# One core: logit sums on GpSimd, conversion steps gathered, a new order at batch ends and tail

## The chip, the cores and the metric

The kernel runs on one core of one Trainium2 chip. The metric is the device time of one execution in microseconds (us), and every time below is in us unless it is marked ns. The engines of a core are TensorE (PE in the profile, its weight loads PEld), VectorE (DVE), ScalarE (ACT), GpSimd (POOL) and SyncE (SP), which here issues the DMAs.

## The reference

Attention with pooled queries, then a soft mixture of experts, then a two-layer block whose activation is a smooth hinge. All tensors are float32.

```
q_pool = q.reshape(B, H, S // 2, 2, D).mean(axis=3)         # B=4, H=8, S=1152, D=64
attn   = softmax(q_pool @ k^T / sqrt(D)) @ v                # 576 rows per head
x      = attn, heads side by side                           # 2304 tokens x 512

logits = x @ phi                                            # 32 slots: 8 experts x 4
d      = softmax(logits, over tokens);   c = softmax(logits, over slots)
slot   = d^T @ x                                            # 32 x 512
so[e]  = relu(slot[e] @ w1[e]) @ w2[e]                      # w1 512 x 1024, w2 1024 x 512
y      = c @ so                                             # 2304 x 512

h = y @ w_in                                                # 512 x 2048
g = 0 below -1, h above 1, (h + 1)^2 / 4 between
out = g @ w_out                                             # 2048 x 512
```

## The kernel before

**Attention.** The 32 heads (4 batches of 8) are worked off in 16 pairs, P = 0 to 15, the two heads of a pair in the two halves of the PE array. The 1152 keys are 9 blocks of 128, so step g = 9 P + c is block c of pair P, and each step has two half-slots (one for each head). In a half-slot TensorE makes the scores in fp16 for the maximum (tile `mx`, L311, four products), the exact scores (`st`, L377) and, for an earlier block, exp times values (`acc`, L409). VectorE takes the row maximum of `mx` (`mp`, L323), ScalarE the exponential (`e`, L382). VectorE also adds the exponentials of several blocks (`es_add`, L390; which ones, in which half-slot and how wide is the table ADD), so that one set of products (`es_sum`, L402) makes the sums of a pair at its end; `es_sum` is the first thing in the trace that belongs to the start of the next pair.

In the same half-slots stand the preparation of later pairs (table PREP): loads of k and q, splits into two fp16 parts (L266, L279, L289 on VectorE), transposes by DMA (L272, L294, L360), a copy of the transposed q to the other 64 partitions (`dup_q1`, L297, a DMA), and, between them, the conversion of the last block's weights (`cv_step`: L207, L209, L212, L215, four steps on VectorE for each piece of 512 columns; table CVS says in which half-slots of a pair they go). After a pair its outputs are transposed and multiplied by phi (`t_x`, L449), scaled (`t_raw`, `t_ev`, `t_mul` on ScalarE) and left in `XL`: for each head and each of five token blocks 64 values and 32 logits.

**Batch end.** A batch is four pairs. In the third pair after its last one, the logits of its eight heads are added (`lg_red`, L489, three reductions on VectorE), then their maximum over tokens is found (`lg_mx`, `lg_tr`, `lg_max`), spread over the partitions (`lg_rep`), exponentiated (`lg_exp`) and multiplied with the tokens (`p_mm`), and the running sums are updated (`p_add`). The last batch does the same behind the last pair, with no attention left beside it.

**Order.** Nothing is reordered behind the code: `plan()` puts each step into a half-slot with `at(g, slot, f, ...)`, the half-slots are emitted in turn, and each engine and each DMA queue works its instructions in the order in which they were emitted. All loads go through SP's queue.

**Tail.** Behind the last batch's chain come the slot inputs (`sT`), the first layer of the experts (`h1`, L741; its 16 weight tiles of 1 MB are w1[e, x]; w1[1, 0] is loaded last, as `w_last`, into memory that the batch chain has to free), the softmax over slots on VectorE (`c_soft`, L763 to L774), the second layer (`s2o`, L798, weights w2), and the product of its result with `w_in` (`M`, L905, then `Mr`, `Mst`).

**Output stage.** For groups of tokens k: `c_xpose(k)` (tile `ct`, L786) makes the transposed coefficients, `h_unit` multiplies them with M (`h`, L927), ScalarE and VectorE form the hinge (`g_unit`, L935 to L948; the first ones in `first_unit`, L973 to L980, where GpSimd subtracts in L980), and `o_part` multiplies with w_out (`po`, L991). The tiles `h` and `ct` share four PSUM buffers.

Of the kernel before, what the change touches and what calls it, by code (L numbers as in the profile page):

```python
# [19 lines left out]
WARM = 2, 2, 3, 2, 6, 3  # L20
# [5 lines left out]
CVS = ((0, 0), (0, 0), (0, 1), (1, 1)), ((0, 0), (0, 0), (0, 1)), ()  # L26
# [7 lines left out]
ADD = (((5, 1, 0, 0, 2), (6, 1, 1, 0, 2), (7, 2, 1, 0, 1), (8, 2, 0, 0, 1), (8, 2, 1, 1, 2), (9, 2, 0, 1, 2),  # L34
        (10, 3, 1, 0, 2), (11, 3, 0, 0, 2), (12, 4, 0, 0, 1), (13, 4, 0, 1, 2), (13, 4, 1, 0, 1), (14, 4, 1, 1, 2), (15, 5, 0, 0, 2),
# [3 lines left out]
PREP = (-20, -18, (-34, -33), -36, -16, -30), (-24, -22, (-37, -36), -37, -17, -32)  # L39
# [3 lines left out]
def fused_kernel(ctx: ExitStack, tc: tile.TileContext, q, k, v, phi, w1, w2, w_in, w_out, out):  # L43
# [420 lines left out]
    def t_last(P, part):  # L464
        def px(h, t):
            i, k = place(t, h)
            return tx[P][:, i, BW * k:BW * k + BW]

        for h in range(2):
            for t in range(NTT):  # L470
                sc = ss[P][:, h, t:t + 1]
                if part == 0:
                    x = LG[:, NTT * (P // HPB) + t, :]
                    nc.vector.scalar_tensor_tensor(out=x, in0=px(h, t)[:, D:BW], scalar=sc, in1=x, op0=ALU.mult, op1=ALU.add)
                elif part == 1 and 2 <= t:
                    nc.scalar.activation(out=xl_of(P, h, t)[:, 0:D], in_=px(h, t)[:, 0:D], func=AF.Copy, scale=sc)
                elif part == 2 and t < 2:
                    nc.vector.tensor_scalar(out=xl_of(P, h, t)[:, 0:D], in0=px(h, t)[:, 0:D], scalar1=sc, scalar2=None, op0=ALU.mult)
# [130 lines left out]
    with tc.manual_schedule():  # L609
# [117 lines left out]
        def over_slots(ps, src):  # L727
            for dc in range(4):
# [32 lines left out]
        def c_soft(i):  # L761
# [55 lines left out]
        c_soft(0)
        for i in range(3):
            if i:
                h1(4 + i, 0)  # L820
            c_soft(1 + i)
        nc.gpsimd.memset(hz1, 0.0)
        h1(7, 0)
        nc.scalar.activation(out=h1s[0], in_=h1p[0][:, 0], func=AF.Copy)
        h1(0, 1)
        h1(1, 1)
        h1(2, 1)
# [53 lines left out]
        nc.vector.tensor_copy(S2sb, s2)  # L881
# [162 lines left out]
        m_rep(0)  # L1044
        w_hi(0, 0)
# [11 lines left out]
        for k in range(len(SEQ)):  # L1057
            if k:
                pos = o_tiles(k)
            if k == 0:  # L1060
# [12 lines left out]
                c_xpose(3)  # L1073
# [79 lines left out]
```

## Time and profile before

| | |
|---|---|
| median of 3 runs | 768.32 us (764.88 to 768.39) |
| profiled execution | 767.93 us, of which its span 766.2 us |
| granted TensorE clock, mean | 0.982 |
| busy: PE, DVE, ACT, POOL | 731.4 (95%), 595.4 (78%), 460.9 (60%), 108.0 (14%) |
| chain of work that ended last | PE 58%, DVE 30%, issue 5%, DMA 4%, ACT 2% |

The span is the time from the first instruction to the last in the trace; the time of the execution is 1.7 us longer. An engine's share of busy time is a mean over stages with different limits, and TensorE's busy time counts a product as longer when its input or its turn comes late. The chain is followed back from the last instruction, at each step to what released it.

### The profile page before, as it was taken

Reading aid. Unit: us, or ns where it says so; the run is one execution under the profiler, and the core shown is the slowest. Engines: PE = TensorE matmul, PEld = TensorE weight load, DVE = VectorE, ACT = ScalarE, POOL = GpSimd, SP = SyncE. Lnnn points to the kernel's source line nnn. Section 1 sums busy time; section 2 is a strip of 40 time slices with the busy share of each in tenths; the row PEclk is TensorE's granted clock in tenths of the full one; section 3 lists DMA queues with packets and bytes.
Section 4 is the critical chain, followed back from the end, with each engine's and each line's share of the span. In section 5 each row is a group of like instructions: output and inputs, shape, how many; then the busy total and the mean of one; then the engine's idle time right before and its main releaser. Section 6 shows DMA issues by size and latency. Waiting matters only on the chain.

```text
span 766.2 us, 19663 instructions
## 1 busy us (share of the span) xinstructions
PE 731.4 (95%) x8138; PEld 569.4 (74%) x8138; DVE 595.4 (78%) x1104; ACT 460.9 (60%) x880; POOL 108.0 (14%) x78
## 2 busy tenths in 40 slices
PE   7789999999999998999999999799899999999998
PEld 6567788786787786788866786524788888888887
DVE  6889898889899889889879778432666798887542
ACT  4245667656667756657755568112878678667650
POOL 7100000000000000000000000001434434335350
PEclk9899999999999999999999999799999999999999
DMA  9698499766598876559775567997101220210122
GB/s 217 124 229 191 111 224 225 155 184 173 133 205 222 159 173 181 132 149 246 151 165 121 160 212 241 345 385 293 55 1 53 86 79 32 83 56 1 58 94 97
DMA packets 135258, 118.75 MB, mean 155 GB/s; under 512 B 81153, under 2 KB 99841, under 8 KB 134657
## 3 DMA queue, kind: packets, MB, share of 16 engines
q1 hardware_dynamic: 135168, 117.50, 58.3%
q8 instruction: 64, 1.05, 0.6%
q14 instruction: 26, 0.20, 0.1%
HBM read 82.90 MB, written 8.91 MB: 120 GB/s over the span
## 4 chain that ended last, share of the span: by engine, by line
PE 58%; DVE 30%; issue 5%; DMA 4%; ACT 2%; SPq 1%; DVEq 0%; ACTq 0%
PE po L991 25%; DVE mp L323 12%; DVE es L390 10%; PE st L377 7%; PE acc L409 6%; PE acc L402 5%; PE tx L449 4%; PE mx L311 3%; PE h L927 2%; PE s2o L798 2%; PE h L741 1%; DMA q<-q 1%; DMA w_last<-in_moe_w_dram 1%; DVE qn L289 1%; DVE xT L489 1%
## 5 line engine op out<-in xcount | busy, mean ns | idle before, releaser
L382 ACT ACTIVATE e<-st 128x576 f32<-128x576 f32 x288 | 187.2, 651 | 118.6 <-PE st L377 104.2
L323 DVE TENSOR_REDUCE mp<-mx 128x1 f32<-128x576 f32 x282 | 210.7, 749 | 43.2 <-PE mx L311 42.4
L409 PE MATMUL acc<-e,vf 128*64 128x288 f32 x1152 | 201.4, 408 | 1.6 <-ACT e L382 1.6
L311 PE MATMUL mx<-K,q 128*64 128x288 f16 x1152 | 125.6, 291 | 11.2 <-DVE mp L323 4.3
L377 PE MATMUL st<-q,K 128*64 128x288 f16 x1152 | 129.3, 288 | 7.4 <-DVE mp L323 5.5
L377 PE MATMUL st<-q,S 128*64 128x288 f16 x1152 | 129.4, 286 | 0.1
L311 PEld LDWEIGHTS <-q 128*64 128x64 f16 x1152 | 76.4, 111 | 64.4 <-issue 8.3
L991 PE MATMUL po<-whi,ghi 128*128 128x512 f32 x280 | 110.2, 394 | 0.0
L991 PE MATMUL po<-wlo,ghi 128*128 128x512 f32 x280 | 110.2, 394 | 0.0
L991 PE MATMUL po<-whi,glo 128*128 128x512 f32 x280 | 110.0, 393 | 0.0
L390 DVE TENSOR_TENSOR es<-es,e 128x288 f32<-128x288 f32 (+1 forms) x190 | 103.9, 560 | 0.0
L960 POOL TENSOR_TENSOR glo<-r,ghi 128x1024 fp32r<-128x1024 f32 x34 | 81.8, 2406 | 118.8 <-DVE r L948 76.6
L377 PEld LDWEIGHTS <-K 128*64 128x64 f16 x1152 | 74.4, 109 | 26.5 <-issue 16.1
L409 PEld LDWEIGHTS acc<-e,vf 128*64 128x64 f32 x1152 | 82.9, 137 | 9.3 <-ACT e L382 4.4
L377 PEld LDWEIGHTS <-S 128*64 128x64 f16 x1152 | 75.9, 110 | 1.3 <-issue 0.4
L1003 DVE TENSOR_TENSOR pa<-po,pa 128x512 f32<-128x512 f32 (+1 forms) x54 | 36.9, 682 | 39.7 <-PE po L991 39.5
L720 POOL MEMSET xT<- 128x1024 f32 x1 | 1.0, 957 | 461.5 <-PE tx L449 461.5
L991 PEld LDWEIGHTS po<-whi,glo 128*128 128x128 f32 x280 | 52.9, 189 | 11.8
L991 PEld LDWEIGHTS po<-whi,ghi 128*128 128x128 f32 x280 | 52.9, 189 | 11.1 <-ACT cl L945 0.2
L991 PEld LDWEIGHTS po<-wlo,ghi 128*128 128x128 f32 x280 | 52.9, 189 | 10.2
L948 DVE SCALAR_TENSOR_TENSOR r<-h,cl 128x512 f32<-128x512 f32 x68 | 43.6, 682 | 8.5 <-ACT cl L944 6.9
L462 ACT ACTIVATE xl<-xl,ss 128x96 f32<-128x96 f32 x150 | 47.1, 366 | 0.0
(185 smaller groups left out, 860.1 us busy)
## 6 DMA issues: line engine op xcount, KB each, us to landing
w<-in_moe_w_dram SPq DMA_DIRECT2D x76, 256.0 KB, 4.5
w<-in_moe_w_dram SPq DMA_DIRECT2D x12, 1024.0 KB, 11.5
vf<-in_v_dram SPq DMA_DIRECT2D x16, 576.0 KB, 4.3
kf<-in_k_dram SPq DMA_DIRECT2D x30, 288.0 KB, 4.0
f<-in_moe_w_in_dram SPq DMA_DIRECT2D x16, 512.0 KB, 4.9
f<-in_moe_w_out_dram SPq DMA_DIRECT2D x16, 512.0 KB, 3.7
qf<-in_q_dram SPq DMA_DIRECT2D x30, 256.0 KB, 5.0
S<-K SPq DMA_DIRECT2D x16, 288.0 KB, 4.7
```

The costliest lines, as they stand in the source:

```text
L311: nc.tensor.matmul(ps[p0:p1, i, 0:HQ], lhsT=q1[P][:, t, p0:p1], rhs=kk[:, j * HQ:(j + 1) * HQ], start=True, stop=True)
L323: nc.vector.tensor_reduce(out=mp[P][:, t, a:a + 1], in_=ps[:, :, 0:HQ], op=ALU.max, axis=AX.XY)
L377: nc.tensor.matmul(ps[c0:c0 + 64, i, 0:HQ], lhsT=kk[:, ci, c0:c0 + 64], rhs=f[:, sl[i]], start=first, stop=not first)
L382: nc.scalar.activation(out=e, in_=ps[:, :, 0:HQ], func=AF.Exp, scale=ESC)
L390: nc.vector.tensor_tensor(out=Es[P, n, h][:, i0:i1], in0=a[:, i0:i1], in1=b[:, i0:i1], op=ALU.add)
L402: nc.tensor.matmul(acc[P, h][32 * r:32 * r + 32, HQ:HQ + SW], lhsT=ones.to_broadcast([128, 32]), rhs=a, start=False, stop=False, skip_grou ...
L409: nc.tensor.matmul(acc[P, i][h * 64:(h + 1) * 64, 0:HQ], lhsT=vt[P][:, h, c, :], rhs=E[P, c, h][:, i, :], start=(c == 0), stop=(c == NK - ...
L462: nc.scalar.activation(out=x, in_=x, func=AF.Copy, scale=ss[P][:, h, t:t + 1])
L948: nc.vector.scalar_tensor_tensor(out=r[:, a:a + 2], in0=ps[a // 2], scalar=-1.0, in1=cl[:, a:a + 2], op0=ALU.max, op1=ALU.add)
L960: nc.gpsimd.tensor_tensor(out=glo[k], in0=r, in1=ghi[k].bitcast(F32), op=ALU.subtract)
L991: nc.tensor.matmul(ps, lhsT=a, rhs=b, start=st_, stop=sp)
L1003: nc.vector.tensor_tensor(out=t, in0=po, in1=t, op=ALU.add)
```

## The change

- The sum of the logits over a batch's heads (`lg_red`, three VectorE reductions per batch) is gone. In its place `lg_add` runs on GpSimd once for each pair but the last: three instructions for a batch's first pair, four for the others. The mask `dupm` is added there too, so `lg_exp` has one VectorE instruction instead of two. `lg_mx` to `lg_exp` stand one half-slot later.
- CVS: the four conversion steps of a pair stand in its first half-slot; before they were spread over three. Pairs from 9 on had three steps, now four.
- ADD: 12 instead of 14 additions for the same blocks, the first one half-slot earlier.
- PREP and `plan`: the loads of q are emitted one half-slot later, the low part of q one later.
- Behind the last pair, `t_last` makes head 0's logits on VectorE, head 1's outputs and head 0's values on ScalarE, and adds with two VectorE instructions; filling products (`warm`) are more or in other places.
- At the start, the memory fills of `S2b` and `qn2b` are divided otherwise between VectorE and GpSimd.
- In the tail `h1` uses `w_last` behind twelve other tiles instead of four, and `c_soft`'s last two steps run on ScalarE and GpSimd.
- `c_xpose(3)` moves from behind group 0's products to right behind `m_rep(0)`; the copy of `S2sb` is shared by VectorE and ScalarE.

```diff
-WARM = 2, 2, 3, 2, 6, 3
+WARM = 8, 4, 4, 2, 6, 3, 4, 2
-CVS = ((0, 0), (0, 0), (0, 1), (1, 1)), ((0, 0), (0, 0), (0, 1)), ()
+CVS = ((0, 0),) * 4, ((0, 0),) * 4, ()
-PREP = (-20, -18, (-34, -33), -36, -16, -30), (-24, -22, (-37, -36), -37, -17, -32)
+PREP = (-20, -18, (-34, -33), -36, -16, -30), (-24, -22, (-37, -36), -37, -17, -31)
...
-    def lg_red(b, i, n):
-        if i < 2:
-            x = XL[:, 0:n, NTT * i:NTT * i + 4, D:BW].rearrange("p c (u h) s -> p u s c h", u=2)
-            o = LG[:, NTT * b + 2 * i:NTT * b + 2 * i + 2, :]
+    def lg_add(P):
+        b, hp = divmod(P, HPB)
+        x = XL[:, hp].rearrange("p (i k) d -> p i k d", i=2)
+        xs = [x[:, :, 0:4, D:BW].rearrange("p i (u h) s -> p h i u s", h=2)[:, h] for h in range(2)]
+        o = LG[:, NTT * b:NTT * b + 4].rearrange("p (i u) s -> p i u s", i=2)
+        o4 = LG[:, NTT * b + 4]
+        x4 = [x[:, h, 4, D:BW] for h in range(2)]
+        add = nc.gpsimd.tensor_tensor
+        if hp == 0:
+            add(out=o, in0=xs[0], in1=xs[1], op=ALU.add)
+            add(out=o4, in0=x4[0], in1=x4[1], op=ALU.add)
+            m = LG[:, NTT * b + 1:NTT * b + NTT]
+            nc.gpsimd.tensor_scalar(out=m, in0=m, scalar1=dupm, scalar2=None, op0=ALU.add)
         else:
-            x = XL[:, 0:n, 4:2 * NTT:NTT, D:BW].rearrange("p c h s -> p s c h")
-            o = LG[:, NTT * b + 4, :]
-        nc.vector.tensor_reduce(out=o, in_=x, op=ALU.add, axis=AX.XY)
+            for h in range(2):
+                add(out=o, in0=o, in1=xs[h], op=ALU.add)
+                add(out=o4, in0=o4, in1=x4[h], op=ALU.add)
...
-                at(b + lk, 0, (load_k2, load_q)[h], P)
+                at(b + lk, h, (load_k2, load_q)[h], P)
...
-                          (lg_mx, q_), (t_last, P, 1), (lg_tr, q_), (warm, WARM[5]),
-                          (t_last, P, 2), (lg_max, q_), (lg_rep, q_), (warm, WARM[1]), (lg_exp, q_), (warm, WARM[2]),
-                          (p_mm, q_), (p_add, q_)):
+                          (lg_mx, q_), (lg_tr, q_), (warm, WARM[5]), (lg_max, q_), (lg_rep, q_), (warm, WARM[1]), (lg_exp, q_),
+                          (p_mm, q_), (warm, WARM[6]), (p_add, q_)):
...
+        at(g0 + 3, 1, lg_add, P)
...
-            eng = nc.gpsimd if i else nc.vector
-            eng.memset(qn2b[i][:, :, D:2 * D], 0.0)
-            eng.memset(S2b[i][64:128], 0.0)
+            nc.vector.memset(S2b[i][64:128], 0.0)
+        for i in range(2):
             nc.gpsimd.memset(S2b[i][64:65], MS)
+            nc.gpsimd.memset(qn2b[i][:, :, D:2 * D], 0.0)
...
-                nc.vector.tensor_copy(CN[:, :, r, :].bitcast(F32R), lgN)
-                nc.vector.tensor_tensor(out=CN[:, :, r + 1, :], in0=lgN, in1=CN[:, :, r, :], op=ALU.subtract)
+                nc.scalar.activation(out=CN[:, :, r, :].bitcast(F32R), in_=lgN, func=AF.Copy)
+                nc.gpsimd.tensor_tensor(out=CN[:, :, r + 1, :], in0=lgN, in1=CN[:, :, r, :], op=ALU.subtract)
...
-        h1(0, 0)
-        h1(2, 0)
-        h1(3, 0)
-        h1(4, 0)
+        for e in (0, 2, 3):
+            h1(e, 0)
+        c_soft(0)
+        for e in (4, 5, 6, 7):
+            h1(e, 0)
+        c_soft(1)
+        for e in range(4):
+            h1(e, 1)
         h1(1, 0)
...
         m_rep(0)
+        c_xpose(3)
         w_hi(0, 0)
...
-                c_xpose(3)
                 continue
```

SP's queue in the first pairs, where q of pair 2 is transposed (L294), copied to the other partitions (L297), and q of the pair after it is loaded (L243 to L246). Before:

```order
L294 DMA_TRANSPOSE q_2_478<-qn_110 128x9x128
L235 DMA kf_523<-in_k_dram 128x576 x2
L243 DMA qf_526<-in_q_dram 128x4x128
L244 DMA qf_526<-in_q_dram 128x4x128
L245 DMA qf_526<-in_q_dram 64x128
L246 DMA qf_526<-in_q_dram 64x128
L297 DMA q_2_478<-q_2_478 64x1152
```

Of the changed kernel:

```order
L294 DMA_TRANSPOSE q_2_480<-qn_110 128x9x128
L235 DMA kf_523<-in_k_dram 128x576 x2
L297 DMA q_2_480<-q_2_480 64x1152
L243 DMA qf_547<-in_q_dram 128x4x128
L244 DMA qf_547<-in_q_dram 128x4x128
L245 DMA qf_547<-in_q_dram 64x128
L246 DMA qf_547<-in_q_dram 64x128
```

The copy L297 now stands ahead of the four loads of q; the two loads of k stay ahead of it.

VectorE at the start of an ordinary pair (`mp` are the maxima, `wst` the piece under conversion, L432 to L436 the reciprocal sums of the pair before). Before:

```order
L266 SCALAR_TENSOR_TENSOR kn_1059<-kf_969,kn_1059 128x9x64
L207 TENSOR_SCALAR wst_73<-wst_73 128x512
L209 TENSOR_SCALAR wst_73<-wst_73 128x512
L323 TENSOR_REDUCE mp_1128<-mx_2_1_1294 128x1
L212 SCALAR_TENSOR_TENSOR wst_73<-f_1_75,wst_73 128x512
L323 TENSOR_REDUCE mp_1128<-mx_3_0_1317 128x1
L432 STREAM_TRANSPOSE xT<-es_0_0_946 128x320
L434 TENSOR_SCALAR ss_1338<-xT 128x10
L436 RECIPROCAL ss_1338<-ss_1338 128x10
L323 TENSOR_REDUCE mp_1128<-mx_3_1_1344 128x1
L215 SCALAR_TENSOR_TENSOR wst_73<-f_1_75,wst_73 128x512
```

Of the changed kernel:

```order
L266 SCALAR_TENSOR_TENSOR kn_1056<-kf_967,kn_1056 128x9x64
L207 TENSOR_SCALAR wst_73<-wst_73 128x512
L209 TENSOR_SCALAR wst_73<-wst_73 128x512
L212 SCALAR_TENSOR_TENSOR wst_73<-f_1_75,wst_73 128x512
L215 SCALAR_TENSOR_TENSOR wst_73<-f_1_75,wst_73 128x512
L323 TENSOR_REDUCE mp_1124<-mx_2_1_1294 128x1
L323 TENSOR_REDUCE mp_1124<-mx_3_0_1316 128x1
L432 STREAM_TRANSPOSE xT<-es_0_0_922 128x320
L434 TENSOR_SCALAR ss_1337<-xT 128x10
L436 RECIPROCAL ss_1337<-ss_1337 128x10
L323 TENSOR_REDUCE mp_1124<-mx_3_1_1343 128x1
```

L212 and L215 now stand ahead of the pair's maxima; before, each stood between two of them.

TensorE where the output stage begins (`Mr` is M spread over the array, `ct` the transposed coefficients of a group, `warm_o` filling products). Before:

```order
L786 MATMUL ct_8410<-ident,CN 128x128 x4
L915 MATMUL Mr_0_8417<-Mhl,Sel 128x256 x2
L915 MATMUL Mr_1_8422<-Mhl,Sel 128x256 x2
L849 MATMUL warm_o<-ident 128x128 x2
L927 MATMUL h_0_8437<-cT,Mst_8416 128x256
```

Of the changed kernel:

```order
L794 MATMUL ct_8429<-ident,CN 128x128 x4
L921 MATMUL Mr_0_8436<-Mhl,Sel 128x256 x2
L921 MATMUL Mr_1_8441<-Mhl,Sel 128x256 x2
L794 MATMUL ct_8446<-ident,CN 128x128 x4
L854 MATMUL warm_o<-ident 128x128 x2
L933 MATMUL h_0_8462<-cT,Mst_8435 128x256
```

The fourth `ct` stands ahead of the first `h`; before, it stood 35 rows further on, behind group 0's products.

## Rows read from the trace of the kernel before

**Rows 1.** Windows: two pairs, an ordinary one and one with a batch end.
```profile
core 0: us, PE busy (x) PEld busy (x) DVE busy (x) ACT busy (x) POOL busy (x), PEclk, DMA share, GB/s
87.64:114.70 27.06, 26.85 (x409) 21.64 (x404) 24.76 (x46) 18.69 (x38) 0.00 (x0) 1.00 0.83 196
168.83:200.70 31.87, 30.09 (x450) 22.24 (x446) 26.78 (x51) 19.08 (x39) 0.00 (x0) 1.00 0.56 141
```
**Rows 2.** Timeline of TensorE, ordinary pair: start, length, instruction.
```profile
90.28 0.41 PE L311 MATMUL mx<-K,q 128*64 128x288 f16 x4
...
92.72 0.41 PE L311 MATMUL mx<-K,q 128*64 128x288 f16 x4
...
100.54 0.44 PE L311 MATMUL mx<-K,q 128*64 128x288 f16 x4
```
**Rows 3.** Timeline of VectorE, same pair; in brackets the idle time before.
```profile
90.73 0.76 DVE L323 TENSOR_REDUCE mp<-mx 128x1 f32<-128x576 f32 x1 [2.13 <-PE mx L311]
91.41 0.68 DVE L212 SCALAR_TENSOR_TENSOR wst<-f,wst 128x512 int32<-128x512 int32 x1
...
93.55 0.70 DVE L323 TENSOR_REDUCE mp<-mx 128x1 f32<-128x576 f32 x1
94.16 0.68 DVE L215 SCALAR_TENSOR_TENSOR wst<-f,wst 128x512 int32<-128x512 int32 x1
```
**Rows 4.** Groups of VectorE, the sums over heads.
```profile
L489 DVE TENSOR_REDUCE xT<-xl 128x64 f32<-128x512 f32 x6 | 6.3, 1046 | 0.0
...
L489 DVE TENSOR_REDUCE xT<-xl 128x32 f32<-128x256 f32 x3 | 1.8, 605 | 0.0
```
**Rows 5.** Timeline of TensorE, its two waits for a copy of q.
```profile
54.58 0.44 PE L311 MATMUL mx<-K,q 128*64 128x288 f16 x4 [1.92 <-DMA q<-q]
...
388.94 0.44 PE L311 MATMUL mx<-K,q 128*64 128x288 f16 x4 [1.55 <-DMA q<-q]
```
**Rows 6.** Timeline of SP, ahead of the first of these waits.
```profile
46.95 0.38 SPq L243 DMA_DIRECT2D qf<-in_q_dram  x1
...
49.18 0.54 SPq L297 DMA_DIRECT2D q<-q  x1
```
**Rows 7.** Timeline of GpSimd and VectorE at the start.
```profile
7.37 2.01 POOL L620 MEMSET S<- 1x2304 f16 x1
...
7.49 2.07 DVE L286 COPY qn<-qn 128x576 f16<-128x576 f16 x1 [0.75 <-ACT qn L282]
```
**Rows 8.** The chain that ended last, around the end of the last pair.
```profile
473.31 1.22 DVE xT L489 x2
...
486.46 0.86 DVE xl L478 x4
```
**Rows 9.** Timeline of TensorE in the tail, first expert layer.
```profile
496.75 5.64 PE L741 MATMUL h<-w,xT 128*32 128x512 f32 x32 [0.45 <-DVE xT L735]
503.43 1.06 PE L741 MATMUL h<-w_last,xT 128*32 128x512 f32 x8 [1.04 <-DMA w_last<-in_moe_w_dram]
504.31 5.33 PE L741 MATMUL h<-w,xT 128*32 128x512 f32 x48
```
**Rows 10.** Windows: three microseconds of the tail, columns as in rows 1.
```profile
497.00:500.00 3.00, 3.00 (x16) 0.59 (x12) 2.13 (x4) 0.74 (x1) 0.00 (x0) 0.50 1.05 388
```
**Rows 11.** The last weight load: SP's timeline, DMA issues (us to landing), TensorE's timeline.
```profile
512.10 2.61 SPq L137 DMA_DIRECT2D w<-in_moe_w_dram  x1
...
w<-in_moe_w_dram SPq DMA_DIRECT2D x1, 1024.0 KB, 14.1
...
528.30 1.04 PE L798 MATMUL s2o<-w,xT 128*32 128x512 f32 x8
```
**Rows 12.** Timeline of TensorE and the chain, first groups of the output stage.
```profile
547.28 0.47 PE L927 MATMUL h<-cT,Mst 128*128 128x256 f32 x2 [2.07 <-DVE r L948]
...
547.75 4.30 PE po L991 x12
...
561.91 2.79 PE po L991 x12
```
**Rows 13.** Groups of GpSimd, its subtractions in the first output units.
```profile
L980 POOL TENSOR_TENSOR glo<-r,ghi 128x256 fp32r<-128x256 f32 x4 | 3.0, 738 | 14.5 <-ACT ghi L979 14.5
...
L980 POOL TENSOR_TENSOR glo<-r,ghi 128x512 fp32r<-128x512 f32 x2 | 2.5, 1282 | 1.0 <-ACT ghi L979 1.0
```

More of the change, by code (lines that the diff above doesn't have):

```diff
@@ L462, in t_mul, with t_last @@
         nc.scalar.activation(out=x, in_=x, func=AF.Copy, scale=ss[P][:, h, t:t + 1])
-    def t_last(P, part):
+    def t_last(P, part=0):
         def px(h, t):
@@ L467, in px @@
             return tx[P][:, i, BW * k:BW * k + BW]
-        for h in range(2):
+        if part == 0:
             for t in range(NTT):
[L471 to L478, printed above, removed]
@@ L480, in fused_kernel @@
-    bt = {}
-    def lg_red(b, i, n):
-        if i < 2:
-            x = XL[:, 0:n, NTT * i:NTT * i + 4, D:BW].rearrange("p c (u h) s -> p u s c h", u=2)
-            o = LG[:, NTT * b + 2 * i:NTT * b + 2 * i + 2, :]
-        else:
-            x = XL[:, 0:n, 4:2 * NTT:NTT, D:BW].rearrange("p c h s -> p s c h")
-            o = LG[:, NTT * b + 4, :]
-        nc.vector.tensor_reduce(out=o, in_=x, op=ALU.add, axis=AX.XY)
+                x = LG[:, NTT * (P // HPB) + t, :]
+                nc.vector.scalar_tensor_tensor(out=x, in0=px(0, t)[:, D:BW], scalar=ss[P][:, 0, t:t + 1], in1=x, op0=ALU.mult, op1=ALU.add)
@@ new lines, in t_last @@
+            for h, n in ((1, BW), (0, D)):
+                for t in range(NTT):
+                    nc.scalar.activation(out=xl_of(P, h, t)[:, 0:n], in_=px(h, t)[:, 0:n], func=AF.Copy, scale=ss[P][:, h, t:t + 1])
+            b, x = P // HPB, XL[:, P % HPB].rearrange("p (i k) d -> p i k d", i=2)
+            o = LG[:, NTT * b:NTT * b + 4].rearrange("p (i u) s -> p i u s", i=2)
+            nc.vector.tensor_tensor(out=o, in0=o, in1=x[:, :, 0:4, D:BW].rearrange("p i (u h) s -> p h i u s", h=2)[:, 1], op=ALU.add)
@@ new lines, in t_last @@
+            o = LG[:, NTT * b + 4]
+            nc.vector.tensor_tensor(out=o, in0=o, in1=x[:, 1, 4, D:BW], op=ALU.add)
+    bt = {}
+    def lg_add(P):
+        b, hp = divmod(P, HPB)
+        x = XL[:, hp].rearrange("p (i k) d -> p i k d", i=2)
+        xs = [x[:, :, 0:4, D:BW].rearrange("p i (u h) s -> p h i u s", h=2)[:, h] for h in range(2)]
+        o = LG[:, NTT * b:NTT * b + 4].rearrange("p (i u) s -> p i u s", i=2)
+        o4 = LG[:, NTT * b + 4]
[6 more added lines that the diff above has]
+            nc.gpsimd.tensor_scalar(out=m, in0=m, scalar1=dupm, scalar2=None, op0=ALU.add)
+        else:
+            for h in range(2):
+                add(out=o, in0=o, in1=xs[h], op=ALU.add)
+                add(out=o4, in0=o4, in1=x4[h], op=ALU.add)
@@ L514, in lg_exp @@
         rep = bt["rep"][:, 0, 0:NS]
-        nc.vector.scalar_tensor_tensor(out=dn[:, 1:NTT], in0=LG[:, NTT * b + 1:NTT * b + NTT, :], scalar=dupm,
-                                       in1=rep.unsqueeze(1).to_broadcast([128, NTT - 1, NS]), op0=ALU.add, op1=ALU.add)
-        nc.vector.tensor_tensor(out=dn[:, 0], in0=LG[:, NTT * b, :], in1=rep, op=ALU.add)
+        nc.vector.tensor_tensor(out=dn, in0=LG[:, NTT * b:NTT * b + NTT, :], in1=rep.unsqueeze(1).to_broadcast([128, NTT, NS]),
+                                op=ALU.add)
         nc.scalar.activation(out=dn, in_=dn, func=AF.Exp)
@@ L596, in plan @@
         if P % HPB == HPB - 1:
-            for s, f, *a in ((7, lg_red, 0, HPB), (8, lg_red, 1, HPB), (9, lg_red, 2, HPB), (9, lg_mx), (11, lg_tr), (11, lg_max), (13, lg_rep),
-                             (13, lg_exp), (16, p_mm), (16, p_add)):
+            for s, f, *a in ((10, lg_mx), (12, lg_tr), (12, lg_max), (14, lg_rep), (14, lg_exp), (16, p_mm), (16, p_add)):
                 at(g0 + s // 2, s % 2, f, q_, *a)
@@ L741, in h1 @@
                 nc.tensor.matmul(h1p[x][32 * dc:32 * dc + 32, 0, :], lhsT=sTz[:, e, dc, :], rhs=wt["w1", e, x][:, dc, :],
-                                 start=(e == 0), stop=(e == E_ - 1))
+                                 start=(e == 0), stop=(e == (E_ - 1 if x else 1)))
             w_used(("w1", e, x))
@@ L809, in divisors @@
             nc.vector.tensor_scalar(out=st4, in0=st4, scalar1=rc4, scalar2=None, op0=ALU.mult)
-        h1(0, 0)
-        h1(2, 0)
-        h1(3, 0)
-        h1(4, 0)
+        for e in (0, 2, 3):
[6 more added lines that the diff above has]
+            h1(e, 1)
         h1(1, 0)
+        nc.scalar.activation(out=h1s[0], in_=h1p[0][:, 0], func=AF.Copy)
         CN = x_p.tile([128, XW], F32, tag="xn", name="CN")[:, 0:NTK * 4 * NS].rearrange("p (n r s) -> p n r s", n=NTK, r=4)
[L817 to L821, printed above, removed]
-        nc.gpsimd.memset(hz1, 0.0)
[L823 to L827, printed above, removed]
+        c_soft(2)
+        c_soft(3)
+        nc.gpsimd.memset(hz1, 0.0)
         divisors()
-        h1(3, 1)
+        h1(4, 1)
         ht_mm(0)
         ht_sum(0)
-        for e in range(4, E_):
+        for e in range(5, E_):
             h1(e, 1)
@@ L879, in fused_kernel @@
             s2o(e, 1)
-        nc.vector.tensor_copy(S2sb, s2)
+        nc.vector.tensor_copy(S2sb[:, 0:256], s2[:, 0:256])
+        nc.scalar.activation(out=S2sb[:, 256:512], in_=s2[:, 256:512], func=AF.Copy)
         c_first()
```

7 lines of the change are left out of this document (3 added, 4 removed).

## The prediction

> **What bounds the kernel now.** I read the page's busy shares and chain first: TensorE is busy 95% of the span, and VectorE is the only other engine with much of the chain. Since a product that waits for its input counts as busy, I then cut attention into windows from one `es_sum` to the next [rows 1]. An ordinary pair takes 27.06 us, TensorE busy 26.85, VectorE 24.76: both are nearly full. A pair with a batch end takes 31.87, 4.81 more, of which TensorE's busy time grows by 3.24 and its idle time by 1.57 (1.78 against 0.21). The timelines of one ordinary pair show which of the two leads. TensorE brings the first maxima's products 1.22 us apart ((92.72 - 90.28) / 2) [rows 2]. VectorE takes the first maximum 0.45 us behind its product (90.73 against 90.28), the third 0.83 behind (93.55 against 92.72) [rows 2, 3]. From there TensorE goes at 1.30 us a half-slot (7.82 us for six): it has run out of free score buffers and is paced by VectorE, which costs six times 0.08, 0.5 us a pair. Yet VectorE sat idle for 2.13 us just before the pair's first maximum [rows 3]. So in attention a microsecond off VectorE is worth time in some half-slots and nothing in others. Last I read the waits of TensorE outside that rhythm: two for a copy of q, one for `w_last`, one at the start of the output stage [rows 5, 9, 12]. Behind the first groups of the output stage TensorE has no wait, and the change touches nothing there.
>
> **The change part by part.** All of it is set against the profiled execution, 767.93 us, which is 0.39 below the median of the runs; durations come from this one trace.
>
> *Start.* VectorE's copy L286 took 2.07 us, and ended when GpSimd's fill that had begun at 7.37 was over (7.37 + 2.01 = 9.38, the copy until 9.56) [rows 7]. The fills are now divided so that this one comes first. A VectorE instruction over 512 columns takes 0.68 [rows 3]; I take that for the copy and gain 2.07 - 0.68 = 1.4. Bounds: 0.3, if the first loads hold the scores anyway, and 1.4.
>
> *Loads of q behind the copy of q.* In two pairs TensorE stood 1.92 and 1.55 us for the duplicate [rows 5]. SP issued it at 49.18, behind four loads of q of which the first went out at 46.95 [rows 6]; now the four loads are behind it. That is 2.23 us earlier in the queue, more than either wait, and four transfers fewer ahead of it. Gain 3.5; at least 1.6 (one of the waits) if the transposes ahead of it are the late ones. The loads themselves come a half-slot later, and are used many half-slots on: nothing.
>
> *Conversions in the first half-slot, and the sums on GpSimd.* L212 and L215 take 0.68 each [rows 3] and now stand where VectorE was idle for 2.13 us, which holds both. VectorE then has only the reciprocal sums between its first three maxima, and can win back most of its 0.38 of lag behind the third before the wide additions begin. I take 0.4 of the 0.5 us for seven ordinary pairs up to 8, where two steps move, and 0.2 for four later ones, where one moves and one is added: 3.6; bounds 0 and 3.6. Against it stands `lg_add`. No row of before has such an instruction; the nearest are L980's, 0.738 us for 256 columns and 1.282 for 512 [rows 13]. The line through them gives, as an estimate, 0.47 for 128 and 0.26 for 32, so four instructions 1.46 us a pair, and 15 pairs (four of them with three instructions, some 1.2) 20.9 us of GpSimd. GpSimd is idle in attention [rows 1], and whoever reads the sums comes three half-slots later, 3.7 us. So it costs nothing unless it holds VectorE. Bounds: nothing and 20.9. The start shows that VectorE can be held by GpSimd (L286), but most of VectorE's time here is maxima out of PSUM; I take a tenth, 0.15 a pair, 2.2 in all. Net gain 1.4.
>
> The Trainium skill, page "SBUF — State Buffer", section "Who interferes with whom", says that a VectorE instruction with two inputs in SBUF contends with a GpSimd instruction that reads SBUF, and that in the modes that use both of VectorE's ports the one that comes second is blocked until the first is through. L286's length agrees for a copy beside a fill; no row of before shows a sum on GpSimd beside VectorE's `es_add`. By that rule up to all of the 20.9 us could fall on VectorE, and the net would be a loss of 17.3 instead of a gain of 1.4.
>
> *Batch ends.* Three reductions leave VectorE, 2 x 1.05 + 0.60 = 2.70 us at each of three batch ends [rows 4]; the merged `lg_exp` saves little and is put at nothing. A batch end costs 4.81 us over an ordinary pair, of which TensorE's idle 1.57 is certainly not its own work [rows 1]; the other 3.24 hold its extra products as well as slow ones. Bounds: 1.57 and 2.70 a batch; I take 2.2, since VectorE paces the pair: 6.6 in all (4.7 to 8.1).
>
> *Last pair.* Of `lg_red` 1.22 us lay on the chain ahead of the last exponentials [rows 8]. Gain 1.2; 0 if the additions behind it were late anyway.
>
> *Tail.* The first 32 products of `h1` ran in 5.64 us, at a granted clock of 0.50, that is at 1.2 GHz; 48 later ones in 5.33, so that 32 would take 3.55 [rows 9, 10]. TensorE waited before it, and for 1.04 us for `w_last` [rows 9]. With filling products ahead of `h1` and `w_last` used later, 2.09 + 1.04 could go, and 0.86 of L478, which is gone from the chain [rows 8]: 4.0. But the weights cap this: transfers ran at 388 GB/s [rows 10], the last weight was issued at 512.10 and landed 14.1 later, at 526.2, and its products started at 528.30 [rows 11]. With nothing loaded sooner TensorE can come 2.1 us earlier and no more; the loads of `h1`'s memory are issued as TensorE frees it, so a part of them does come sooner. I take 2.5; bounds 0 and 4.0.
>
> *Start of the output stage.* With the fourth `ct` out of the way, the third group's `h` needs no buffer that VectorE is still reading. The wait of 2.07 goes, and the 12 products behind it, which took 4.30 where later ones take 2.79, lose nothing to a low clock: 2.07 + 1.51 = 3.6 [rows 12]; bounds 2.1 (the clock falls anyway) and 3.6.
>
> Sum: 1.4 + 3.5 + 1.4 + 6.6 + 1.2 + 2.5 + 3.6 = 20.2; 767.93 - 20.2 = **747.7 us**.
>
> **Rivals.**
>
> *A, the other side: GpSimd's sums hold VectorE.* Place: wherever `lg_add` runs beside `es_add` and the splits of q and k, late in a pair, when VectorE paces TensorE. Without any such cost the change gains 22.4. It is used up when each of 15 pairs loses 1.49 us, and the kernel is slower by half a per cent (3.84 us, about what a measurement of this kernel can tell from no change) from 1.75 us on. At the estimated 1.46 fully waited for, the time is 767.9 - 22.4 + 20.9 = 766.4. For it: L286 [rows 7]. Against it: in [rows 1] the pair is not VectorE's alone, so it would have to pass on every microsecond, and the price itself would have to be higher than the line through [rows 13]. The Trainium skill's rule above is this rival's.
>
> *B: the tail gives nothing.* The weights arrive no sooner, TensorE waits for them in `s2o` and its clock falls there for some 2 us: 747.7 + 2.5 + 2 = 752.2. For it: the cap of 2.1 us and the full DMA engines [rows 10, 11].
>
> *C: attention gives little.* The moved conversions free nothing, as VectorE is late again by the additions, and GpSimd costs a third of its price, 0.5 a pair: 767.9 - 18.8 + 7.5 = 756.6.
>
> *D: more.* Batch ends give all 8.1, GpSimd costs nothing, the tail gives 4.0: 747.7 - 1.5 - 2.2 - 1.5 = 742.5.
>
> **How the numbers follow.** The forecast (744.5 to 751) has 0.47, B 0.12, C 0.17, D 0.17, A 0.07 (0.04 within half a per cent, 0.03 slower). The range goes from 740, which is D and some of the 3.5 us by which runs of one kernel differ, to 758, just beyond C; A and the ends of C and D are left out, some 0.15. The chances: faster 0.93, same 0.04, slower 0.03.
>
> **What the profile of the changed kernel would show.** Start: L286 near 0.7. Loads: no wait of TensorE for `q<-q`. Pairs: ordinary ones near 26.7 us, no step of 1.30 between the second and the sixth maxima. GpSimd: `lg_add` near 0.5 and 0.3 an instruction, and `es_add` no longer than before; if those beside `lg_add` are much longer, A or C holds. Batch ends: near 29.5. Tail: `h1`'s first products at a granted clock of 1.00, and no wait for `w_last`; a wait for a w2 tile in `s2o` means B. Output: twelve products in 2.8 from the first group on, no wait for `r`. The forecast is wrong if `lg_add` takes over 3.7 us in a batch's last pair, since `lg_mx` then waits with VectorE's whole queue behind it, or if the first half-slot's four steps hold the first maximum, for which TensorE waits at the pair's start.

## The result, and the profile after

The changed kernel takes 759.76 us (median of 7 runs, 756.85 to 762.46) against 768.29 before; the ratio is 0.9904 [0.9878, 0.9929]. It is faster by 1.0%, not by the 2.6% that was forecast, and 1.8 us above the top of the range. The profiled execution took 759.76 us. One execution of e7 below, 817.81 us at a granted clock of 0.848, is left out of every ratio; it moves e7's median by 0.2 us.

The page of the changed kernel: its span and the chain.

```profile
span 758.0 us, 19766 instructions
...
PE 70%; DVE 14%; DMA 9%; ACT 3%; issue 2%; SPq 1%; POOL 0%; ACTq 0%; DVEq 0%
```

VectorE's share of the chain fell from 30% to 14%. But DMA, 4% before, is now 9%. Where, the lengths of the pairs tell. They are worked out from the timelines of three kernels, each from one first product of `es_sum` to the next (kernel e1 is the first experiment below). A batch end falls into the second pair after the batch's last one, into 5, 9 and 13:

```
pair        to 1   1     2     3     4     5*    6     7     8     9*    10    11    12    13*   14    15    rest
before      60.37 27.09 27.06 27.06 27.07 31.86 27.06 27.06 27.06 32.25 26.73 26.69 29.03 32.14 25.44 24.27 287.96
changed     57.39 29.44 27.74 27.49 26.73 29.78 27.21 26.98 29.34 30.20 29.46 26.87 27.74 30.19 25.33 23.80 282.31
e1          57.12 27.32 26.62 26.73 26.71 29.78 26.62 26.72 26.84 30.18 26.62 26.73 26.72 30.17 26.17 23.80 280.85
                                                                                              * with a batch end
```

The start won 2.98 us, pair 12 with its wait for q 1.29, the three batch ends 6.08, the last pair 0.47, all that follows 5.65: 16.5 us. The ordinary pairs (1 to 4, 6 to 8, 10, 11, 14) lost 8.3, nearly all of it in pairs 1, 8 and 10, where 3.6 less the cost of GpSimd had been expected as a gain. Pairs 5, 9 and 13 hold no conversion step (the third entry of CVS is empty), and their gain came nearly as forecast. The windows of the changed kernel answer to [rows 1]: an ordinary pair that went well, one with a batch end, and pair 8.

```profile
core 0: us, PE busy (x) PEld busy (x) DVE busy (x) ACT busy (x) POOL busy (x), PEclk, DMA share, GB/s
142.06:168.79 26.73, 26.59 (x413) 21.70 (x404) 25.16 (x44) 18.18 (x37) 1.85 (x4) 1.00 0.84 209
168.79:198.57 29.78, 29.55 (x454) 22.20 (x446) 24.25 (x45) 19.09 (x39) 1.85 (x4) 1.00 0.55 141
...
252.76:282.10 29.34, 27.51 (x411) 21.89 (x404) 25.70 (x44) 18.08 (x37) 1.89 (x4) 1.00 0.93 196
```

The first two stand as forecast (near 26.7 and 29.5). In pair 8 TensorE is idle for 1.8 us and stretched for another 0.9 (busy 27.51 against 26.59 in the pair that went well). The waits of TensorE over the whole span (us in total, times, longest) name what it waited for; before, the first was 1.6 in five times, and the second was not there:

```profile
PE acc L409 <- ACT e L382: 4.4, 8, 1.5
...
PE st L377 <- DMA q<-qn: 2.8, 3, 1.6
```

And the chain of the changed kernel through pair 8 (start, length, what):

```profile
266.72 3.30 DMA kf<-in_k_dram
...
270.09 0.06 ACT kn L258
...
274.53 5.51 DMA q<-qn
...
280.08 0.44 PE st L377 x4
```

A load of k came too late. ScalarE, whose split of k (L258) stood in its queue ahead of the next exponential, waited 1.51 us for it, and TensorE for ScalarE. The transposes behind the maximum (L360) then went out 21.77 us into the pair instead of 19.69, took 5.5 us to land instead of 3.2, and TensorE waited for them as well. In this trace ScalarE waits for k in every ordinary pair in which its load goes out 12.69 us or more into the pair (1 to 3, 6 to 8, 10 and 12), and not in pairs 4 and 11, where it goes out at 11.90 and 10.93. So the question is what makes this load late, and that is SP's queue. Its timeline in the kernel before, where pair 8 begins at 254.63:

```profile
251.82 0.49 SPq L300 DMA_DIRECT2D S<-K  x1
253.04 1.31 SPq L272 DMA_TRANSPOSE K<-kn  x1
...
259.37 1.84 SPq L272 DMA_TRANSPOSE K<-kn  x1
262.05 0.33 SPq L218 DMA_DIRECT2D cv_dr<-wst  x1
262.47 0.38 SPq L193 DMA_DIRECT2D f<-in_moe_w_in_dram  x1
...
265.02 1.07 SPq L235 DMA_DIRECT2D kf<-in_k_dram  x2
```

And in the changed kernel, where it begins at 252.76; the last conversion step on VectorE, then SP:

```profile
254.67 0.69 DVE L215 SCALAR_TENSOR_TENSOR wst<-f,wst 128x512 int32<-128x512 int32 x1
...
255.39 0.33 SPq L218 DMA_DIRECT2D cv_dr<-wst  x1
255.81 0.38 SPq L193 DMA_DIRECT2D f<-in_moe_w_in_dram  x1
256.28 0.49 SPq L300 DMA_DIRECT2D S<-K  x1
256.83 2.79 SPq L272 DMA_TRANSPOSE K<-kn  x1
...
260.73 3.34 SPq L272 DMA_TRANSPOSE K<-kn  x1
...
266.72 1.05 SPq L235 DMA_DIRECT2D kf<-in_k_dram  x2
```

`cv_step`'s last step also issues two DMAs: the store of the piece and the load of the next one. Moved to the first half-slot, they came to stand ahead of the fill of S and both transposes of K. The store needs L215, which ends at 255.36, and SP issues it at 255.39. So the fill, which went out 2.81 us ahead of the pair before, goes out 3.52 behind its start, 6.3 us later; then the rest is issued in close succession, the two transposes of K hold SP for 6.13 us instead of 3.15, and the load of k goes out 13.96 us into the pair instead of 10.39.

### The profile page after: what moved, and what is told of

The parts are those of the page before. It is cut to its first block, busy times and chain, and to the rows that moved or that the text cites. A ratio compares the mean times of both kernels' runs of the same rounds, so it can differ in the third digit from the quotient of the medians.

```text
span 758.0 us, 19766 instructions
## 1 busy us (share of the span) xinstructions
PE 728.5 (96%) x8160; PEld 569.8 (75%) x8160; DVE 585.4 (77%) x1047; ACT 463.8 (61%) x887; POOL 138.4 (18%) x136
## 4 chain that ended last, share of the span: by engine, by line
PE 70%; DVE 14%; DMA 9%; ACT 3%; issue 2%; SPq 1%; POOL 0%; ACTq 0%; DVEq 0%
PE po L997 25%; PE st L377 13%; PE acc L409 12%; DVE mp L323 7%; PE mx L311 6%; PE acc L402 4%; DVE es L390 4%; PE tx L449 4%; DMA q<-qn 3%; DMA kf<-in_k_dram 2%; PE h L933 2%; DMA w<-in_moe_w_dram 2%; ACT e L382 2%; DMA w_last<-in_moe_w_dram 2%; PE po L1003 1%
## 5 line engine op out<-in xcount | busy, mean ns | idle before, releaser
L409 PE MATMUL acc<-e,vf 128*64 128x288 f32 x1152 | 209.8, 409 | 4.5 <-ACT e L382 4.4
L311 PE MATMUL mx<-K,q 128*64 128x288 f16 x1152 | 132.6, 291 | 7.4 <-DVE mp L323 4.3
L377 PE MATMUL st<-q,K 128*64 128x288 f16 x1152 | 133.5, 287 | 4.1 <-DVE mp L323 1.0
L377 PE MATMUL st<-q,S 128*64 128x288 f16 x1152 | 133.7, 286 | 2.8 <-DMA q<-qn 2.8
L311 PEld LDWEIGHTS <-q 128*64 128x64 f16 x1152 | 79.0, 111 | 58.0 <-issue 8.4
L390 DVE TENSOR_TENSOR es<-es,e 128x576 f32<-128x576 f32 (+1 forms) x160 | 102.3, 640 | 0.0
L409 PEld LDWEIGHTS acc<-e,vf 128*64 128x64 f32 x1152 | 86.8, 137 | 15.1 <-ACT e L382 10.0
L377 PEld LDWEIGHTS <-K 128*64 128x64 f16 x1152 | 77.7, 109 | 20.6 <-issue 13.8
L377 PEld LDWEIGHTS <-S 128*64 128x64 f16 x1152 | 78.5, 110 | 4.5 <-issue 3.6
L499 POOL TENSOR_TENSOR xT<-xT,xl 128x128 f32<-128x128 f32 x22 | 11.0, 501 | 240.1 <-ACT xl L462 240.0
```

Of the source, the lines that this page charges most:

```text
L311: nc.tensor.matmul(ps[p0:p1, i, 0:HQ], lhsT=q1[P][:, t, p0:p1], rhs=kk[:, j * HQ:(j + 1) * HQ], start=True, stop=True)
L377: nc.tensor.matmul(ps[c0:c0 + 64, i, 0:HQ], lhsT=kk[:, ci, c0:c0 + 64], rhs=f[:, sl[i]], start=first, stop=not first)
L390: nc.vector.tensor_tensor(out=Es[P, n, h][:, i0:i1], in0=a[:, i0:i1], in1=b[:, i0:i1], op=ALU.add)
L409: nc.tensor.matmul(acc[P, i][h * 64:(h + 1) * 64, 0:HQ], lhsT=vt[P][:, h, c, :], rhs=E[P, c, h][:, i, :], start=(c == 0), stop=(c == NK - ...
```

## Experiments

Three theories stood at the beginning. **S**: SP's queue, as just read. **Q**: the loads of q, now behind the copy of q, do the damage, as SP waits at the copy for the transposes and the loads then stand just ahead of L360. **G**: GpSimd's sums hold VectorE. Each group of four kernels ran on one chip, with the kernel before beside it; between the groups the ratios are compared. The experiments' line numbers are shifted by up to 10: the fill of S is L300 here and L306 in e1.

**e1_split**

```diff
-            if n < 16:
-                nc.sync.dma_start(out=cv_dr[:, x, :], in_=dst)
-            if n + 2 < 32:
-                cv_load(n + 2)
+            if dma:
+                cv_dma(n)
...
+            if g < g1_:
+                at(g + CVD[0], CVD[1], cv_dma, n)
...
+CVD = 1, 1
```

`cv_dma` issues the same two DMAs; from step g1_, three ahead of the last pair, on they stay with the conversion.

> The changed kernel, with all four conversion steps still in a pair's first half-slot, but the store of the converted piece and the load of the next one issued three half-slots later, where they stood before the change. Theory S (this store and load, now ahead of the fill of S and the two transposes of K in SP's queue, make the load of k and the transposes behind it late): the waits of 8.5 us in pairs 1, 2, 3, 8 and 10 go, about 751 us. Theory Q (the loads of q behind the copy of q do it): no change, 759.8. Theory G (GpSimd's sums hold VectorE): no change, 759.8.

748.62 us, ratio 0.9767 [0.9741, 0.9793]. This is theory S, and also the lowest ratio of the study (e8 and e12 below can't be told from it): 2.3% faster than before, and faster than the changed kernel by more than both intervals. SP's timeline in e1, where pair 8 begins at 247.62, has the order of before, and the load of k goes out 9.09 us into the pair:

```profile
244.81 0.49 SPq L306 DMA_DIRECT2D S<-K  x1
246.03 1.35 SPq L278 DMA_TRANSPOSE K<-kn  x1
...
252.35 1.70 SPq L278 DMA_TRANSPOSE K<-kn  x1
254.15 0.53 SPq L224 DMA_DIRECT2D cv_dr<-wst  x1
...
256.71 1.52 SPq L241 DMA_DIRECT2D kf<-in_k_dram  x2
```

**e2_loadq**

```diff
-                at(b + lk, h, (load_k2, load_q)[h], P)
+                at(b + lk, 0, (load_k2, load_q)[h], P)
```

> The changed kernel, with the loads of q again emitted with those of k, ahead of the copy of q. Theory Q: the waits for the transposes and for k go, 8.5 us less, while the two waits for the copy come back with 3.5, about 755 us. Theory S: the waits stay and 3.5 us come on top, about 763 us. Theory G: 763 us.

773.57 us, 1.0078 [1.0048, 1.0108]. Q falls: without that move the changed kernel would have been slower than before. S had the sign, not the size. TensorE's waits in e2 show why: the copy of q, behind late transposes and four loads, is late in ten pairs instead of two.

```profile
PE mx L311 <- DMA q<-q: 15.1, 10, 2.4
```

**e3_cvs**

```diff
-CVS = ((0, 0),) * 4, ((0, 0),) * 4, ()
+CVS = ((0, 0), (0, 0), (0, 1), (1, 1)), ((0, 0), (0, 0), (0, 1)), ()
```

> The changed kernel, with the conversion steps again spread over three half-slots of a pair, their store and load with them. Theory S: as without the early store, but without what VectorE wins by the early steps, 751 to 755 us. Theories Q and G: 759.8, or a little more.

753.16 us, 0.9824 [0.9792, 0.9857], as S has it. Undoing the edit makes the changed kernel faster. From e3 to e1, on the same chip, the early steps without their DMAs are worth 4.5 us by the medians, but of the 3.8 us between the two traces only 2.3 lie in the pairs, where the steps are; 2.3 lie behind the last pair, and the start is 0.9 the other way. The prediction's term was 3.6.

**e4_vsum**: `lg_red` with its three reductions per batch, and `lg_exp` as before; no `lg_add`.

```diff
-        at(g0 + 3, 1, lg_add, P)
...
+            for s, f, *a in ((7, lg_red, 0, HPB), (8, lg_red, 1, HPB), (9, lg_red, 2, HPB), (10, lg_mx), (12, lg_tr), (12, lg_max), ...
```

> The changed kernel, with the sums over heads again as three reductions on VectorE at a batch end, none on GpSimd. Theory G: ordinary pairs get shorter by the 8.5 us that the change lost there, batch ends longer by the 6 that it won, about 757 us. Theories S and Q: only the 6 us of three batch ends and 0.8 of the last pair come back, about 766.5 us.

764.64 us, 0.9966 [0.9947, 0.9986]. G falls: without GpSimd's sums the kernel is 4.8 us slower by the ratios, and its ordinary pairs still have the waits.

The next four ask what in SP's queue costs, the wait for VectorE or the bytes moved beside the transposes, and what two other edits are worth without the disturbance.

**e5_store_early**, against e1:

```diff
-                at(g + CVD[0], CVD[1], cv_dma, n)
+                at(g + CVD[0][0], CVD[0][1], cv_store, n)
+                at(g + CVD[1][0], CVD[1][1], cv_next, n)
...
-CVD = 1, 1
+CVD = (0, 0), (1, 1)
```

> As the kernel with both transfers late (748.6 us), but the store of the converted piece stands in the first half-slot again, ahead of the fill of S; the load of the next piece stays late. If what costs is that SP waits there for VectorE's last conversion step with the fill and the transposes behind it (hold), all of the 11 us come back, about 759.8. If it is the traffic of the two transfers beside the transposes, a third of it does (256 of 768 KB), about 752.

761.41 us, 0.9906 [0.9877, 0.9934]: all of it is back, with a third of the bytes.

**e6_load_early**, against e5:

```diff
-CVD = (0, 0), (1, 1)
+CVD = (1, 1), (0, 0)
```

> The other half: the load of the next piece in the first half-slot, which waits for the same conversion step, since it overwrites what that step reads; the store late. Hold: all of the 11 us, about 759.8. Traffic: two thirds (512 of 768 KB), about 756.

757.61 us, 0.9857 [0.9832, 0.9883]. By the ratios 6.9 of 10.5 us come back, which alone would speak for the bytes. But the smaller transfer of e5 costs all 10.5, so bytes are not the measure. Why the wait of the load costs less than that of the store stays open.

**e7_split_vsum**: e1's edit and e4's together.

> Both transfers late, and the sums over heads on VectorE as before the change, none on GpSimd: what GpSimd's sums are worth where SP does not disturb. The prediction's terms: 6.6 for the batch ends and 1.2 for the last pair, less 2.2 for holding VectorE, 5.6, so about 754 us. If GpSimd holds VectorE by its whole time, 20.9 us, it would be faster than with the sums on GpSimd, about 735.

754.21 us, 0.9811 [0.9783, 0.984]. GpSimd's sums are worth 3.4 us by the ratios, with an uncertainty of nearly the same size; in the trace its three batch ends and its last pair are 6.0 us longer than e1's.

**e8_split_loadq**: e1's edit and e2's together.

> Both transfers late, and the loads of q again ahead of the copy of q: what that move is worth where SP does not disturb. The prediction's term: 3.5 us, so about 752 us, with the waits for the copy in two pairs. If the move matters as much as it did with the early transfers (13.8 us), about 762.

751.57 us, 0.9773 [0.9743, 0.9803]: by the ratios 0.5 us behind e1, with intervals that leave room for the expected 3.5. Not resolved. In its trace TensorE waits 3.0 us for the copy of q, in e1 not at all; 2.1 of them lie ahead of pair 1, which starts at 61.64 instead of 57.12. Pair 12, where the kernel before had its second wait for q, takes 26.72 us as in e1, although the four loads stand ahead of the copy again.

**e9_hold_only**, against e1:

```diff
+    def cv_hold(n):
+        _, dst, x = cv[n]
+        nc.sync.dma_start(out=cv_dr[0:16, x, 0:8], in_=dst[0:16, 0:8])
...
+                at(g, sl, cv_hold, n)
                 at(g + CVD[0], CVD[1], cv_dma, n)
```

> Both transfers late, and in the first half-slot, where the store stood, a store of 512 bytes of the same piece: SP waits for VectorE's last conversion step as in the changed kernel, but nearly nothing is moved there. If the wait in SP's queue is what costs, the 11 us come back, about 759 us; if it is the bytes beside the transposes, it stays near 748.6.

762.21 us, 0.9933 [0.9912, 0.9953]. 512 bytes cost at least as much as the whole store and load. Pairs 1, 2, 6 and 10 take 28.6 to 29.3 us. Pair 10 begins at 312.25; the last conversion step on VectorE, then SP, then ScalarE:

```profile
314.76 0.69 DVE L216 SCALAR_TENSOR_TENSOR wst<-f,wst 128x512 int32<-128x512 int32 x1
...
315.48 0.33 SPq L223 DMA_DIRECT2D cv_dr<-wst  x1
315.90 0.49 SPq L310 DMA_DIRECT2D S<-K  x1
316.49 1.68 SPq L282 DMA_TRANSPOSE K<-kn  x1
...
324.11 1.52 SPq L245 DMA_DIRECT2D kf<-in_k_dram  x2
...
329.42 0.68 ACT L268 ACTIVATE kn<-kf 128x576 f16<-128x576 f32 x1 [1.56 <-DMA kf<-in_k_dram]
```

SP issues nothing from 304.83 on until VectorE's step ends at 315.45. The fill goes out 3.65 us into the pair; in e1 it goes out 3.18 ahead of pair 10. The load of k goes out at 11.86 instead of 8.88, and ScalarE waits for it as in pair 8 of the changed kernel. The transposes of K hold SP for 1.68 and 1.31 us here, so their longer hold in the changed kernel is not needed for the loss. A pair is the longer the later its fill: 26.7 and 27.3 us where the fill goes out 2.05 and 2.12 us into the pair (11 and 8), 28.0 and 28.7 at 3.05 and 3.09 (12 and 2), 28.6 to 29.3 from 3.65 on (6, 10 and 1).

**e10_before_cvs**: the kernel before with the change's CVS line alone.

> The kernel before with the early conversions alone, their store and load with them, all else as before. By the waits in SP's queue: slower than before. From the kernel with the loads of q put back (773.6), plus the 13.6 us that start, batch ends, last pair, tail and output stage gained in the changed kernel, about 787 us. By the prediction's own term for this edit, faster by 3.6: 764.

790.21 us, 1.0296 [1.0276, 1.0317]. Alone, the edit that was booked as a gain of 3.6 us costs 22.7.

**e11_later**, against e1:

```diff
-CVD = 1, 1
+CVD = 4, 0
```

> Both transfers five half-slots later still (in the ninth half-slot of the pair), behind the loads of q: if it is enough that they stand behind the transposes of K, no change from 748.6; if they also hold up the transposes of q and the load of k where they are now, up to 3 us less.

754.84 us, 0.9847 [0.9821, 0.9874]: slower than e1, which neither expectation had. TensorE's waits in e11 show the place: the transposes of L360, which come next in the queue there, are now late in six pairs.

```profile
PE st L383 <- DMA q<-qn: 5.1, 6, 1.7
```

**e12_ct_back**, against e1:

```diff
         m_rep(0)
-        c_xpose(3)
...
                 nc.sync.dma_start(out=Wst[:, 0:4, :], in_=cv_dr[:, 12:16, :])
+                c_xpose(3)
                 continue
```

> Both transfers late, and the fourth transposed coefficients made behind group 0's products again. The prediction's term: 3.6 us (bounds 2.1 and 3.6), so about 752 us. The trace of the changed kernel suggests less, since from the end of the second expert layer to the end it is only 2.1 us shorter than before.

749.75 us, 0.9779 [0.9753, 0.9804]: 0.9 us by the ratios, whose intervals leave room for none and for the 3.6; 2.3 by the spans of the two profiles (745.7 and 748.0), of which 2.1 lie behind the second expert layer (236.83 against 234.72). The timeline and the chain of e12 have back what [rows 12] showed,

```profile
529.11 0.73 PE L942 MATMUL h<-cT,Mst 128*128 128x256 f32 x2 [2.07 <-DVE r L963]
...
529.83 4.10 PE po L1006 x12
```

and the next group starts at 533.77 instead of 529.27 in e1. But e1 then meets waits that e12 does not, 0.51 us for `r` and 0.78 for M's second half, here in e1's timeline:

```profile
542.68 1.00 PE L942 MATMUL h<-cT,Mst 128*128 128x256 f32 x4 [0.51 <-DVE r L963]
...
548.47 0.74 PE L930 MATMUL Mr<-Mhl,Sel 128*128 128x256 f32 x4 [0.78 <-DVE Mhl L923]
```

Behind them the products stand at 549.21 and 551.49 (e1 and e12): of 4.5 us won, 2.3 are left.

## Why the prediction was wrong

The step that failed is the third, *conversions in the first half-slot*. It counted L212 and L215 as VectorE instructions that move into idle time, and that part holds: in pair 4 of the changed kernel TensorE's maxima come 1.22 us apart up to the eighth, but for one step of 1.28, where [rows 2] had 1.30 on the mean from the third on, and the pair takes 26.73 us instead of 27.07. It did not follow the last step's own DMAs into SP's queue, although the order of that queue was read for the loads of q. The store waits for VectorE at a place where, of what is queued behind it, the fill and the first transpose of K had gone out before the pair began, and the second 4.74 us into it (7.97 in the changed kernel).

The trace of before shows the same hold in two pairs. From pair 9 on CVS gave a pair three steps, so that the last step of a piece came into the first half-slot of pairs 11 and 12. Here SP in pair 12, which begins at 367.36:

```profile
369.07 0.33 SPq L218 DMA_DIRECT2D cv_dr<-wst  x1
...
369.97 0.49 SPq L300 DMA_DIRECT2D S<-K  x1
...
380.31 1.05 SPq L235 DMA_DIRECT2D kf<-in_k_dram  x2
```

The fill goes out 2.61 us into the pair, the load of k 12.95, ScalarE waits 1.2 us for k, and the second wait for the copy of q [rows 5] follows. The prediction put that wait down to the loads of q; in e8 they stand as before, the hold is gone, and so is the wait.

The terms, from the pair lengths and timelines; `tail` ends with the last product of `s2o`:

| step | predicted | changed kernel | e1 |
|---|---|---|---|
| start, and the first wait for q | -1.4 -1.9 | -3.0 | -3.3 |
| second wait for q, pair 12 | -1.6 | -1.3 | -2.3 |
| ordinary pairs, GpSimd's cost included | -1.4 | **+8.3** | -1.2 |
| three batch ends | -6.6 | -6.1 | -6.1 |
| last pair | -1.2 | -0.5 | -0.5 |
| tail | -2.5 | -3.5 | -5.0 |
| output stage | -3.6 | -2.1 | -2.1 |
| sum | -20.2 | -8.2 | -20.5 |

The trace of e1 is that of its fastest execution. By the medians of one chip e1 is 18.2 us faster than the kernel before (748.62 against 766.85), where 20.2 had been forecast. So with the two DMAs left where they were the sum was nearly right, and one entry had the wrong sign. In part that is luck: in e1 the tail and the second wait for q gave 3.2 us more than their terms, the batch ends, the last pair and the output stage 2.7 less. Point by point:

- *Start.* L286 now takes 0.33 us instead of 2.07; 0.68 was assumed.
- *Loads of q.* Both waits of TensorE for `q<-q` are gone, the second for another reason than the one given (above). What was not seen is that this move protects the copy when its transposes are late: 13.4 us by the ratios of e2 and the changed kernel.
- *GpSimd's price.* The larger groups of GpSimd's sums in the changed kernel, and the four sums of one pair from its timeline:

```profile
L500 POOL TENSOR_TENSOR xT<-xT,xl 128x32 f32<-128x32 f32 x22 | 11.9, 543 | 19.2 <-ACT xl L462 19.2
L499 POOL TENSOR_TENSOR xT<-xT,xl 128x128 f32<-128x128 f32 x22 | 11.0, 501 | 240.1 <-ACT xl L462 240.0
L496 POOL TENSOR_SCALAR xT<-xT,cols 128x128 f32<-128x128 f32 x4 | 4.3, 1070 | 0.4
```

```profile
124.63 0.46 POOL L499 TENSOR_TENSOR xT<-xT,xl 128x128 f32<-128x128 f32 x1 [23.93 <-ACT xl L462]
126.73 0.25 POOL L500 TENSOR_TENSOR xT<-xT,xl 128x32 f32<-128x32 f32 x1 [1.65 <-ACT xl L462]
126.94 0.46 POOL L499 TENSOR_TENSOR xT<-xT,xl 128x128 f32<-128x128 f32 x1
127.36 0.82 POOL L500 TENSOR_TENSOR xT<-xT,xl 128x32 f32<-128x32 f32 x1
```

  The line through [rows 13] gave 0.47 and 0.26, and most sums took 0.46 and 0.25. The second sum of 128 x 32 of a pair, right behind the sum before it, took 0.72 to 0.82, and the mask's `tensor_scalar` 1.07 by the mean. In all, with 2.8 us for the first sums of the batches, it is 30.0 us, not 20.9. In a batch's last pair the four stretch over 3.6 us (178.84 to 182.41), their waits for ScalarE included. That is just under the 3.7 that the prediction named, and VectorE does not wait for them.
- *Does it hold VectorE?* The wide additions of `es_add`, in e1 with GpSimd's sums and in e7 without (mean ns last):

```profile
L396 DVE TENSOR_TENSOR es<-es,e 128x576 f32<-128x576 f32 x100 | 75.5, 755 | 0.0
L396 DVE TENSOR_TENSOR es<-e,e 128x576 f32<-128x576 f32 x32 | 24.8, 775 | 0.0
```

```profile
L396 DVE TENSOR_TENSOR es<-es,e 128x576 f32<-128x576 f32 x100 | 74.7, 748 | 0.0
L396 DVE TENSOR_TENSOR es<-e,e 128x576 f32<-128x576 f32 x32 | 23.9, 747 | 0.0
```

  That is 1.7 us of VectorE (the changed kernel and e4 differ likewise, 755 and 776 ns against 749 and 748), where 2.2 us of the kernel's time were taken; less of it shows there, since ordinary pairs without a wait take 26.62 us in e7 and 26.62 to 26.73 in e1. Rival A had a true mechanism and a small size. The Trainium skill, page "SBUF — State Buffer", section "Who interferes with whom", has such an addition contend with a sum on GpSimd; the trace agrees in kind, with 1.7 us on VectorE for 30 us of GpSimd.
- *Batch ends and last pair.* 6.1 of 6.6, and 0.5 of 1.2; e7 gives nearly the same from the other side (6.0 for both).
- *Tail.* From the last pair's `es_sum` to the first product of `h1` it was 18.5 us (478.24 to 496.75) and is 14.8 (475.69 to 490.46). Then the weights bind, as feared: the timeline of the changed kernel has `h1` at full rate, 9.65 us for 88 products at a granted clock of 1.00, a wait of 0.38 us for `w_last` behind them (1.04 before), and its last products of `s2o` waiting.

```profile
490.46 9.65 PE L749 MATMUL h<-w,xT 128*32 128x512 f32 x88
...
522.20 1.06 PE L806 MATMUL s2o<-w,xT 128*32 128x512 f32 x8 [1.62 <-DMA w<-in_moe_w_dram]
```

  `h1` and `s2o` together take 32.8 us (to 523.26), 32.6 before. The wait that rival B named is there, 2.3 us in two pieces, but the granted clock did not fall, as the window of the changed kernel with both pieces shows:

```profile
518.80:523.30 4.50, 2.24 (x21) 0.48 (x18) 0.15 (x2) 0.00 (x0) 0.00 (x0) 1.00 1.03 420
```

  From the last pair's `es_sum` to the last product of `s2o` it was 51.1 us and is 47.6, a gain of 3.5 where 2.5 was taken.
- *Output stage.* 3.6 was too much: the wait of 2.07 and the slow products went, but part was given back at the next groups' waits (e12), and 2.1 are left, the lower bound.

## What to carry to other kernels

A step that is moved takes its DMAs with it, and a DMA that waits for a compute engine holds what stands behind it in its queue (e9: the fill went out 6.8 us later, seen from the pair's start): before moving it, list what stands behind the new place and when that used to go out. When such a step has idle time to use on its engine, move the computation and leave the DMA behind (e1: 10.5 us by the ratios). Read each edit's effect stage by stage, since a net gain of 8 us was here, by the traces, one of 20 and a loss of 12.

## What the runs showed of the hardware

- A store of 512 bytes that waits in SP's queue cost at least as much as the full transfers of 768 KB at the same place (ratios 0.9933 and 0.9904, against 0.9767 with nothing there).
- The time that SP spends on a transposing DMA is not fixed: the transposes of K held it for 1.31 and 1.84 us in a pair of the kernel before, for 2.79 and 3.34 in pair 8 of the changed kernel, where they were issued right behind other transfers.
- On GpSimd a sum of 128 x 32 took 0.25 us behind a wait, and 0.72 to 0.82 right behind a sum of 128 x 128; whether waiting for that one is counted in it, the traces don't tell.
